# Attention and two MLP layers in one kernel: layer 2 eleven pairs behind layer 1 instead of fifteen, two slot orders, key sums on VectorE alone

## The chip, the core and the metric

The program runs on one core of a Trainium2 chip. The metric is the device time of one execution in microseconds (us). The core has five engines with queues of their own: TensorE (PE, with its weight loads shown apart as PEld), VectorE (DVE), ScalarE (ACT), GpSimd (POOL) and SyncE (SP), which here only issues DMAs. Each engine takes its instructions strictly in the order in which they were written, and an instruction that waits for a semaphore holds up everything behind it on its engine.

## What is computed

```python
kv_pool = kv.reshape(B, H // 4, 4, W // 4, 4, C).mean(axis=(2, 4))   # 12288 rows -> 768 keys
k = v = kv_pool.reshape(B, -1, C) @ w_sr
s = (q @ k.transpose(0, 2, 1)) / np.sqrt(C)
a = np.exp(s - s.max(-1, keepdims=True));  a /= a.sum(-1, keepdims=True) + 1e-09
x = a @ v                                          # 12288 tokens x 128
h = x @ moe_w_in;   x2 = (h * np.clip(h + 3, 0, 6) / 6) @ moe_w_out      # layer 1, d_ff 2048
h = x2 @ moe2_w_in; g = np.where(h >= 1, h, np.where(h <= -1, 0, (h + 1) ** 2 / 4))
out = g @ moe2_w_out                               # layer 2, d_ff 2048
```

The four weight matrices arrive as 64-bit floats, and are turned into 32-bit values on the chip. Every large product is made of three products of a high and a low part (high x high, high x low, low x high), so that each operand is split once into `hi` (a cast on ACT) and `lo` (a subtraction).

## The kernel before

**Units of work.** The 12288 tokens are 24 blocks of 512. In each layer a block has 8 pairs (a pair is 256 columns of d_ff), so that each layer has 192 pairs. A pair of layer 1 is: `m_in(0, s)`, six matmuls on PE into a PSUM tile `h`; `relu1` (ACT); `mul1` (DVE); `hi_lo` (a cast on ACT, a subtraction on POOL); `m_out(0, s)`, six matmuls into the accumulator `acc0`. A pair of layer 2 is: `m_in(1, s)`; `clip2` (DVE, into the buffer `g2`); `sq2` (ACT); `max2` (DVE, the last reader of `h`); `hi_lo` (ACT, POOL); `m_out(1, s)` into `acc1`. There are two `h` tiles and two `g2` buffers. At the end of a block `acc1` is transposed by `o_T` (DVE) and stored; there is one `acc1`, so the next block's first `m_out(1)` waits for `o_T`.

**Attention of a block.** It comes in four parts of 128 queries: `s_mm` (PE), `s_max` (DVE), `s_exp` (ACT), `s_tail_a` (DVE, ACT), `s_tail_b` (DVE and a transposing DMA on SP); `av` (PE) then makes 256 columns of x out of two parts.

**Order.** Nothing is scheduled by a program: the instructions stand as the Python code issues them. First a prologue, a string of steps: `k` sums a tile of 1024 key rows (12 tiles, eight on DVE and four on POOL by `KV_MODE`), `g` finishes the sum on PE, `t p z y` make keys and values, `jN.0` to `jN.3` are the four stages that convert weight piece N (of 16), `s n e a b` are attention of block 0, `x0 x1` its `av`. Then comes one call of `slot(T)` for T = 0, 1, 2, ...: pair T of layer 1, pair T - O2 of layer 2 with O2 = 15, and beside them attention of the next blocks and, at the slots of `CONV_AT`, the conversion of one more weight piece, whose four stages take four slots. `max2` and `hi_lo` of layer 2's pair stand at the start of the next slot. From T = 192 on there is only layer 2. `out2` issues `m_out(1)` two slots behind its `m_in(1)`, and three behind from T = 192 + LAG3_AT on.

**Names and lines** (of the profile): `kv_pool` L235 to L239, `q_T` L325 to L330, `m_in` L416, `m_out` L431, `x2h` and `x2l` L438 and L439, `o_T` L447, `relu1` L460, `mul1` L467, `clip2` L474, `sq2` L481, `max2` L486, `hi_lo` L496 (cast) and L500 (subtraction), `s_tail_b` L379, weight stages L164 to L195.

Of the kernel before, what the change touches and what calls it, by code (L numbers as in the profile page):

```python
# [46 lines left out]
def tile_attn_moe_moe2(  # L47
# [267 lines left out]
    def q_load(b):  # L315
        if b >= NB:
            return
        q_t[b] = q_p.tile([128, BLK], FP32, tag="q", name="q")
# [238 lines left out]
    def slot(T):  # L557
        s1, s2 = T, T - O2
        if ok(s1):
            m_in(0, s1)  # L560
        if ok(s2 - 1) and T < NS:
            max2(s2 - 1)
        if T in tail_at and T > EXP_T:
            s_exp(*tail_at[T])
        if ok(s1):
# [5 lines left out]
        if T < NS:
            out2(T)
        if ok(s1):
            mul1(s1)
# [111 lines left out]
```

## Time and profile before

| | us |
|---|---|
| three runs | 1460.87, 1462.96, 1463.34 (median 1462.96) |
| the profiled execution | 1460.99 |
| its span, first to last instruction | 1459.2 |
| PE, DVE, ACT, POOL busy | 1340.0, 1117.1, 964.2, 1066.1 |

```profile
PE   4658899999999999999999999999999999999665
DVE  7578887778778878878878778788788888766543
ACT  2557777767667667667677677677677677667432
POOL 5267897777777777778778778778778687778433
PEclk9879999999999999999999999999999999999978
DMA  9352222222122122122122212212212212200000
```

Each digit is the busy share of one fortieth of the span (36.5 us) in tenths, 9 being 90% or more; PEclk is the clock that PE was granted, in tenths of full speed. PE is at 9 from the sixth slice to the thirty-seventh; at both ends it is not, and there the clock digit falls as well.

### The profile page before, as it was taken

What the parts mean: (1) busy time and instruction counts of PE and PEld (TensorE: products, weight loads), DVE (VectorE), ACT (ScalarE), POOL (GpSimd) and SP (SyncE); (2) the same over time, 40 slices, a digit from 0 to 9 for tenths busy, and PEclk for the clock granted to TensorE, in tenths of its full rate; (3) what the DMA queues carried; (4) which work ended last, traced back from release to release, by engine and by line L of the source; (5) the groups of instructions that cost most, each with busy time, mean ns of one, the idle gap of its engine ahead of it and who ended that gap; (6) DMA issues with size and microseconds to landing.
All of it is one profiled execution on the core that took longest, in us unless ns stands there. A gap on an engine that the chain in (4) does not pass through costs nothing.

```text
span 1459.2 us, 16720 instructions
## 1 busy us (share of the span) xinstructions
PE 1340.0 (92%) x6123; PEld 1071.1 (73%) x6123; DVE 1117.1 (77%) x1253; ACT 964.2 (66%) x1141; POOL 1066.1 (73%) x485
## 2 busy tenths in 40 slices
PE   4658899999999999999999999999999999999665
PEld 4546677787787787787787787787787787787443
DVE  7578887778778878878878778788788888766543
ACT  2557777767667667667677677677677677667432
POOL 5267897777777777778778778778778687778433
PEclk9879999999999999999999999999999999999978
DMA  9352222222122122122122212212212212200000
GB/s 311 80 119 40 45 46 37 40 40 42 35 40 47 30 40 48 30 40 47 33 37 47 38 32 47 40 30 47 40 30 47 38 24 40 40 12 8 8 7 8
DMA packets 260770, 66.18 MB, mean 45 GB/s; under 512 B 252368, under 2 KB 256592, under 8 KB 260688
## 3 DMA queue, kind: packets, MB, share of 16 engines
q1 hardware_dynamic: 257344, 62.68, 21.8%
q10 hardware_dynamic: 3344, 2.43, 0.6%
q8 instruction: 49, 0.80, 0.2%
q14 instruction: 33, 0.27, 0.1%
HBM read 21.04 MB, written 6.29 MB: 19 GB/s over the span
## 4 chain that ended last, share of the span: by engine, by line
PE 76%; DVE 7%; POOL 3%; ACT 3%; issue 2%; POOLq 0%; DVEq 0%; ACTq 0%
PE acc L431 33%; PE h L416 32%; PE s L342 6%; PE s L394 6%; POOL l L500 3%; DVE g L474 2%; DVE g L486 2%; ACT h L496 1%; DVE o L447 1%; ACT x2h L438 1%; DVE a L379 1%; DVE wa L175 0%; ACT t L460 0%; DVE nm L348 0%; DVE wa L173 0%
## 5 line engine op out<-in xcount | busy, mean ns | idle before, releaser
L500 POOL TENSOR_TENSOR l<-g,h 128x1024 fp32r<-128x1024 f32 (+1 forms) x200 | 459.3, 2298 | 314.9 <-issue 222.0
L500 POOL TENSOR_TENSOR l<-t,h 128x1024 fp32r<-128x1024 f32 (+1 forms) x215 | 531.0, 2474 | 26.8 <-ACT h L496 26.8
L474 DVE TENSOR_SCALAR g<-h 128x1024 f32<-128x1024 f32 (+1 forms) x193 | 234.9, 1218 | 131.5 <-PE h L416 83.6
L467 DVE SCALAR_TENSOR_TENSOR t<-t,h 128x1024 f32<-128x1024 f32 (+1 forms) x193 | 233.9, 1212 | 100.4 <-ACT t L460 100.4
L460 ACT ACTIVATE t<-h 128x1024 f32<-128x1024 f32 (+1 forms) x193 | 196.7, 1020 | 147.0 <-PE h L416 106.1
L481 ACT ACTIVATE g<-g 128x1024 f32<-128x1024 f32 (+1 forms) x193 | 203.6, 1056 | 115.6 <-DVE g L474 114.0
L496 ACT CAST h<-t 128x1024 fp32r<-128x1024 f32 (+1 forms) x193 | 202.1, 1047 | 87.5 <-DVE t L467 84.6
L496 ACT CAST h<-g 128x1024 fp32r<-128x1024 f32 (+1 forms) x193 | 200.4, 1039 | 77.8 <-DVE g L486 75.2
L486 DVE TENSOR_TENSOR g<-h,g 128x1024 f32<-128x1024 f32 (+1 forms) x193 | 232.4, 1205 | 22.6 <-ACT g L481 22.4
L416 PE MATMUL h<-x2h,wi1h 128*128 128x512 f32 x384 | 157.8, 411 | 28.3 <-DVE g L486 25.3
L431 PE MATMUL acc<-h,wo1h 128*128 128x512 f32 x384 | 156.2, 407 | 19.6 <-DVE o L447 18.2
L431 PE MATMUL acc<-l,wo1h 128*128 128x512 f32 x384 | 154.0, 401 | 12.4 <-POOL l L500 12.4
L416 PE MATMUL h<-xh,wi0h 128*128 128x512 f32 x384 | 153.5, 400 | 9.1 <-ACT wi0h L193 8.5
L416 PE MATMUL h<-xh,wi0l 128*128 128x512 f32 x384 | 154.3, 402 | 4.7 <-POOL wi0l L195 4.7
L431 PE MATMUL acc<-l,wo0h 128*128 128x512 f32 x384 | 154.2, 402 | 4.6 <-POOL l L500 4.3
L431 PE MATMUL acc<-h,wo0h 128*128 128x512 f32 x384 | 156.3, 407 | 0.1
L431 PE MATMUL acc<-h,wo1l 128*128 128x512 f32 x384 | 153.9, 401 | 1.4 <-POOL wo1l L195 1.4
L416 PE MATMUL h<-x2l,wi1h 128*128 128x512 f32 x384 | 154.5, 402 | 0.0
L416 PE MATMUL h<-x2h,wi1l 128*128 128x512 f32 x384 | 154.1, 401 | 0.0
L416 PE MATMUL h<-xl,wi0h 128*128 128x512 f32 x384 | 153.8, 400 | 0.0
L431 PE MATMUL acc<-h,wo0l 128*128 128x512 f32 x384 | 152.5, 397 | 0.5 <-POOL wo0l L195 0.5
L379 DVE SCALAR_TENSOR_TENSOR a<-e,rc,a 128x768 f16<-128x768 f32 x96 | 128.6, 1340 | 2.1 <-ACT a L372 2.1
(146 smaller groups left out, 2121.6 us busy)
## 6 DMA issues: line engine op xcount, KB each, us to landing
out_dram<-o SPq DMA_DIRECT2D x96, 64.0 KB, 2.0
q<-in_q_dram SPq DMA_DIRECT2D x92, 64.0 KB, 2.5
h<-in_moe_w_out_dram SPq DMA_DIRECT2D x4, 512.0 KB, 6.5
l<-in_kv_dram SPq DMA_DIRECT2D x4, 512.0 KB, 8.9
h<-in_kv_dram ACTq DMA_DIRECT2D x3, 512.0 KB, 5.5
at<-a SPq DMA_TRANSPOSE x96, 3.6
g<-in_moe_w_in_dram SPq DMA_DIRECT2D x2, 512.0 KB, 5.6
g<-in_kv_dram SPq DMA_DIRECT2D x2, 512.0 KB, 8.7
```

Source lines behind the costliest of these rows:

```text
L342: nc.tensor.matmul(s[:, h, :384], l[:, js], r[:, ks], start=(n == 0), stop=(n == 2))
L379: nc.vector.scalar_tensor_tensor(out=a[:, 1], in0=e, scalar=rc, in1=a[:, 0], op0=ALU.mult, op1=ALU.subtract)
L394: nc.tensor.matmul(ps, l[:, k, :], r[:, k, :], start=(n == 0), stop=(n == 3 * KC - 1))
L416: nc.tensor.matmul(ps[:, k], l[:, ws], r, start=(n == 0), stop=(n == 2))
L431: nc.tensor.matmul(acc[m], l[:, ws], r[:, k, :], start=(c == 0 and i == 0), stop=(c == NPAIR - 1 and i == 5))
L460: nc.scalar.activation(out=g[:, p], in_=h_t[0, s][:, p], func=ACTF.Relu, scale=1.0 / 6.0, bias=0.5)
L467: nc.vector.scalar_tensor_tensor(out=g[:, p], in0=g[:, p], scalar=1.0, in1=h[:, p], op0=ALU.min, op1=ALU.mult)
L474: nc.vector.tensor_scalar(out=g[:, p], in0=h_t[1, s][:, p], scalar1=1.0, scalar2=-1.0, op0=ALU.min, op1=ALU.max)
L481: nc.scalar.activation(out=g[:, p], in_=g[:, p], func=ACTF.Square, scale=0.5, bias=0.5)
L486: nc.vector.tensor_tensor(out=g[:, p], in0=h[:, p], in1=g[:, p], op=ALU.max)
L496: nc.scalar.copy(out=hi[:, p], in_=g[:, p])
L500: eng.tensor_tensor(out=lo[:, p], in0=g[:, p], in1=f32(hi[:, p]), op=ALU.subtract)
```

## The change

- The four key tiles that POOL summed are summed on DVE; the prologue takes the tiles one by one (`k0 g0`, `k1 g1`, ...).
- The queries of block 0 are loaded as plain rows and transposed by four matmuls against the identity into PSUM, with their low part made on DVE; before, they were loaded in pieces of 32 columns and transposed on DVE. Their load stands behind four key tiles instead of ahead of all.
- Weight pieces 4 and 5 are begun in the prologue, and the other ten in slots 0 to 14 (before: 12 pieces in slots 0 to 19).
- O2 is 11 instead of 15. `LAG3_AT` (O2 - 6) and `o_at` follow it.
- Slots 0 to 19 have an order of their own (`early_slot`), in which `max2` stands in its own slot and `m_out(1)` at the slot's end. `slot` serves from 20 on, with `o_T` behind `mul1` instead of at the slot's end, as long as T < 192.
- In the last eleven pairs of layer 2 every second one uses the `t1` buffers for `clip2` instead of `g2`, and from T = 192 on `sq2` stands ahead of `max2` and `hi_lo` of the pair before.

```diff
-O2, LAG2 = 15, 2
+O2, LAG2 = 11, 2
-LOADS = "q0 k0 w k1 k2 k3 w k4 k5 k6 k7 w k8 k9 k10 k11 w q1 w q2 w w w w w w w w w w w"
-KV_MODE = "VVGVVGVVGVGV"
+LOADS = "k0 w k1 k2 k3 q0 w k4 k5 k6 k7 w k8 k9 k10 k11 w w w q1 w w w q2 w w w w w w w"
 PROLOGUE = """
-j0.0 k0 j0.1 k1 k2 g0 g1 t0 p0 j0.2 k3 z0 y0 j1.0 j0.3 k4 k5 g2 g3 t1 p1 j1.1 z1 y1 q0 k6 k7
...
+k0 g0 j0.0 k1 g1 j0.1 t0 p0 k2 z0 y0 g2 j0.2 k3 g3 t1 p1 j1.0 z1 y1 j0.3 k4 g4 q0 k5 g5 t2 p2 j1.1
...
+j2.2 j3.0 j2.3 j3.1 x0 q1 j4.0 x1 j3.2 j4.1 j3.3 j5.0 j4.2
-CONV_AT = (0, 1, 2, 3, 5, 7, 9, 11, 13, 15, 17, 19)
-ACT_T = 24
+CONV_AT = (0, 1, 3, 4, 6, 7, 8, 10, 12, 14)
+EARLY_T = 20
+ACT_T = 20
+ACT_A0 = (0, 1)
...
-        eng = nc.vector if KV_MODE[i] == "V" else nc.gpsimd
-        eng.tensor_tensor(out=t[:, :, 0:2], in0=t[:, :, 0:2], in1=t[:, :, 2:4], op=ALU.add)
+        nc.vector.tensor_tensor(out=t[:, :, 0:2], in0=t[:, :, 0:2], in1=t[:, :, 2:4], op=ALU.add)
...
+        if b == 0:
+            t, tok = new_s()[:, 0], q_t.pop(0)
+            for n in range(4):
+                nc.tensor.transpose(t[:, n * 128:(n + 1) * 128], tok[:, n], ident)
+            nc.scalar.copy(out=hi, in_=t)
+            nc.vector.tensor_tensor(out=lo, in0=t, in1=f32(hi), op=ALU.subtract)
...
     def clip2(s):
-        g = g_t[1, s] = hl_p.tile([128, 2, 512], FP32, tag="g2", name="g2")
+        tag = "t1" if s >= NS - O2 and s % 2 else "g2"
+        g = g_t[1, s] = hl_p.tile([128, 2, 512], FP32, tag=tag, name=tag)
...
+    def early_slot(T):
+        s1, s2 = T, T - O2
+        if ok(s1):
+            m_in(0, s1)
+            relu1(s1)
+        if T in tail_at:
+            s_tail_a(*tail_at[T], on_act=T < ACT_T)
+        mul1(s1)
+        if ok(s2):
+            m_in(1, s2)
+            clip2(s2)
+        if ok(s2 - 1):
+            hi_lo(1, s2 - 1)
+        hi_lo(0, s1)
+        if ok(s2):
+            sq2(s2)
+        if T in s_at:
+            s_mm(*s_at[T])
+            s_max(*s_at[T])
+        if T in tail_at:
+            s_tail_b(*tail_at[T])
+        if ok(s2):
+            max2(s2)
...
+        conv_step(T in CONV_AT)
+        load_next()
+        if ok(s1 - 1):
+            m_out(0, s1 - 1)
+        out2(T)
...
     def slot(T):
...
         if ok(s1):
             mul1(s1)
+        if T in o_at and T < NS:
+            o_T(o_at[T])
         if ok(s2):
             m_in(1, s2)
...
         if ok(s2):
             sq2(s2)
+        if ok(s2 - 1) and T >= NS:
+            max2(s2 - 1)
+            hi_lo(1, s2 - 1)
...
         if T >= NS:
             out2(T)
-        if T in o_at:
-            o_T(o_at[T])
+            if T in o_at:
+                o_T(o_at[T])
```

**Early slots, DVE.** From slot 16 into slot 17 of the kernel before: `t` is `mul1`'s output, `g` that of `clip2` and `max2`, `wa` and `wst` belong to the weight conversion.

```order
L467 SCALAR_TENSOR_TENSOR t_1496<-t_1496,h 128x1024
L474 TENSOR_SCALAR g_1522<-h 128x1024
L348 TENSOR_REDUCE nm<-s 128x1
L173 TENSOR_SCALAR wa<-wa 128x512
L175 TENSOR_SCALAR wa<-wa 128x512
L486 TENSOR_TENSOR g_1522<-h,g_1522 128x1024
L366 TENSOR_SCALAR su<-su 128x1
L369 RECIPROCAL rc<-su 128x1
L467 SCALAR_TENSOR_TENSOR t_1556<-t_1556,h 128x1024
```

The same engine in the changed kernel, from slot 15 into slot 16.

```order
L477 SCALAR_TENSOR_TENSOR t_1284<-t_1284,h 128x1024
L486 TENSOR_SCALAR g_1299<-h 128x1024
L389 SCALAR_TENSOR_TENSOR a<-e,rc,a 128x768
L498 TENSOR_TENSOR g_1299<-h,g_1299 128x1024
L172 TENSOR_SCALAR wa<-wa 128x512
L174 TENSOR_SCALAR wa<-wa 128x512
L477 SCALAR_TENSOR_TENSOR t_1339<-t_1339,h 128x1024
```

`max2` (L486 before, L498 now) stood behind the conversion's DVE instructions and now stands ahead of them.

**Full slots, DVE.** Around an `o_T` (the transpose into `o`) in the middle of the kernel before; `x2l` is the low part of layer 2's input, `nm` is `s_max`.

```order
L467 SCALAR_TENSOR_TENSOR t_5994<-t_5994,h 128x1024
L474 TENSOR_SCALAR g_6018<-h 128x1024
L348 TENSOR_REDUCE nm<-s 128x1
L439 TENSOR_TENSOR x2l<-acc_5643,x2h 128x512
L447 STREAM_TRANSPOSE o<-acc_5595 128x512
L486 TENSOR_TENSOR g_6018<-h,g_6018 128x1024
```

The same in the changed kernel.

```order
L477 SCALAR_TENSOR_TENSOR t_5850<-t_5850,h 128x1024
L457 STREAM_TRANSPOSE o<-acc_5447 128x512
L486 TENSOR_SCALAR g_5880<-h 128x1024
L358 TENSOR_REDUCE nm<-s 128x1
L498 TENSOR_TENSOR g_5880<-h,g_5880 128x1024
```

The transpose has moved ahead of `clip2` and `s_max`, and, as layer 2's block now ends four slots apart from layer 1's, it no longer stands behind `x2l`.

**Last slots, DVE.** `clip2` and `max2` in turn in the kernel before, with the buffers' numbers.

```order
L474 TENSOR_SCALAR g2_11707<-h_11700 128x1024
L486 TENSOR_TENSOR g2_11692<-h_11685,g2_11692 128x1024
L474 TENSOR_SCALAR g2_11729<-h_11722 128x1024
L486 TENSOR_TENSOR g2_11707<-h_11700,g2_11707 128x1024
L474 TENSOR_SCALAR g2_11750<-h_11743 128x1024
```

The same in the changed kernel.

```order
L486 TENSOR_SCALAR g2_11688<-h_11681 128x1024
L498 TENSOR_TENSOR t1_11661<-h_11654,t1_11661 128x1024
L486 TENSOR_SCALAR t1_11703<-h_11696 128x1024
L498 TENSOR_TENSOR g2_11688<-h_11681,g2_11688 128x1024
L486 TENSOR_SCALAR g2_11725<-h_11718 128x1024
```

The order is the same; the outputs take turns between two `g2` and two `t1` buffers.

## Rows read from the trace of the kernel before

**Rows 1.** Windows: us, busy by engine (instructions), PEclk, DMA share, GB/s.

```profile
0.00:60.80 60.80, 32.11 (x135) 27.30 (x135) 40.92 (x71) 21.81 (x43) 23.19 (x24) 0.92 0.83 234
60.80:133.20 72.40, 52.41 (x228) 39.05 (x229) 55.01 (x65) 47.63 (x68) 47.32 (x32) 0.88 0.32 71
133.20:193.60 60.40, 51.35 (x218) 39.03 (x217) 50.71 (x57) 45.06 (x60) 51.05 (x37) 0.92 0.23 44
193.60:279.10 85.50, 81.15 (x380) 64.93 (x379) 68.96 (x76) 60.50 (x71) 70.53 (x40) 1.00 0.21 40
279.10:1350.00 1070.90, 1055.55 (x4945) 854.68 (x4944) 853.68 (x945) 752.16 (x860) 833.17 (x337) 1.00 0.21 37
1350.00:1361.00 11.00, 10.03 (x43) 7.72 (x41) 9.25 (x9) 5.26 (x8) 5.35 (x3) 1.00 0.00 1
1361.00:1439.40 78.40, 46.77 (x150) 30.76 (x150) 32.45 (x29) 26.55 (x28) 30.78 (x13) 0.87 0.04 7
1439.40:1459.20 19.80, 10.63 (x30) 7.66 (x30) 6.08 (x8) 5.25 (x7) 4.75 (x2) 0.76 0.09 14
```

**Rows 2.** Waits of PE, 60 to 224 us: us in total, times, longest.

```profile
PE h L416 <- ACT wi0h L193: 8.5, 2, 4.8
PE h L416 <- DVE g L486: 4.8, 2, 3.8
PE h L416 <- POOL wi0l L195: 4.7, 2, 2.4
```

**Rows 3.** Key sums on DVE by line: ns min/median/max, first and last start.

```profile
L238 DVE TENSOR_TENSOR l<-l x3: 681/1415/1765, 15.6 to 23.3; 128x512 f32<-128x512 f32 x3
...
L239 DVE TENSOR_TENSOR g<-g x3: 424/1371/1400, 8.8 to 31.7; 128x256 f32<-128x256 f32 x3
L239 DVE TENSOR_TENSOR l<-l x3: 424/828/1372, 16.3 to 25.1; 128x256 f32<-128x256 f32 x3
```

**Rows 4.** Timeline of the prologue: start us, us, engine, line, what [idle before <-releaser].

```profile
0.73 2.05 ACTq L320 DMA_DIRECT2D q<-in_q_dram  x4
...
8.07 0.69 DVE L238 TENSOR_TENSOR g<-g 128x512 f32<-128x512 f32 x1 [6.01 <-DMA g<-in_kv_dram]
...
31.66 1.37 DVE L239 TENSOR_TENSOR g<-g 128x256 f32<-128x256 f32 x1
...
60.81 0.50 PE L416 MATMUL h<-xh,wi0h 128*128 128x512 f32 x1 [0.56 <-ACT xh L399]
```

**Rows 5.** Waits of PE, 224 to 1356 us.

```profile
PE acc L431 <- DVE o L447: 15.9, 21, 1.6
```

**Rows 6.** Timeline around one `o_T`, DVE and then PE.

```profile
766.53 1.23 DVE L474 TENSOR_SCALAR g<-h 128x1024 f32<-128x1024 f32 x1 [0.54 <-PE h L416]
...
775.76 0.70 DVE L447 STREAM_TRANSPOSE o<-acc 128x512 f32<-128x512 f32 x1
...
776.61 0.47 PE L431 MATMUL acc<-h,wo1h 128*128 128x512 f32 x1 [0.71 <-DVE o L447]
```

**Rows 7.** Timeline of one pair of layer 2 ahead of T = 192.

```profile
1341.60 0.39 PE L416 MATMUL h<-x2h,wi1h 128*128 128x512 f32 x1
1341.83 0.39 PE L416 MATMUL h<-x2l,wi1h 128*128 128x512 f32 x1
...
1343.28 1.23 DVE L474 TENSOR_SCALAR g<-h 128x1024 f32<-128x1024 f32 x1 [0.55 <-PE h L416]
```

**Rows 8.** Timeline of a slot behind T = 192, all engines.

```profile
1388.65 1.22 DVE L474 TENSOR_SCALAR g<-h 128x1024 f32<-128x1024 f32 x1 [3.69 <-POOL l L500]
...
1389.79 1.21 DVE L486 TENSOR_TENSOR g<-h,g 128x1024 f32<-128x1024 f32 x1
...
1391.09 1.05 ACT L496 CAST h<-g 128x1024 fp32r<-128x1024 f32 x1 [4.04 <-DVE g L486]
...
1391.15 0.47 PE L416 MATMUL h<-x2h,wi1h 128*128 128x512 f32 x1
...
1392.28 2.36 POOL L500 TENSOR_TENSOR l<-g,h 128x1024 fp32r<-128x1024 f32 x1 [3.67 <-ACT h L496]
...
1394.67 1.22 DVE L474 TENSOR_SCALAR g<-h 128x1024 f32<-128x1024 f32 x1 [3.67 <-POOL l L500]
```

**Rows 9.** Timeline of PE at the last pair's `m_in(1)`.

```profile
1440.01 0.63 PE L416 MATMUL h<-x2l,wi1h 128*128 128x512 f32 x1
1440.43 0.63 PE L416 MATMUL h<-x2h,wi1l 128*128 128x512 f32 x1
```

More of the change, by code (lines that the diff above doesn't have):

```diff
@@ L39 @@
 AB = 3
-EXP_T = 11
-HALF_T = 24
 LO_DVE = ((0, 'out', 2),)
@@ L236, in kv_pool @@
         t = kv_t[i][0]
-        eng = nc.vector if KV_MODE[i] == "V" else nc.gpsimd
-        eng.tensor_tensor(out=t[:, :, 0:2], in0=t[:, :, 0:2], in1=t[:, :, 2:4], op=ALU.add)
-        eng.tensor_tensor(out=t[:, :, 0], in0=t[:, :, 0], in1=t[:, :, 1], op=ALU.add)
+        nc.vector.tensor_tensor(out=t[:, :, 0:2], in0=t[:, :, 0:2], in1=t[:, :, 2:4], op=ALU.add)
+        nc.vector.tensor_tensor(out=t[:, :, 0], in0=t[:, :, 0], in1=t[:, :, 1], op=ALU.add)
     def kv_sum_mm(i):
@@ L317, in q_load @@
             return
+        if b == 0:
+            q_t[b] = q_p.tile([128, 4, C], FP32, tag="q", name="q")
+            nc.scalar.dma_start(out=q_t[b], in_=q[0, :BLK].rearrange("(n p) c -> p n c", p=128))
+            return
         q_t[b] = q_p.tile([128, BLK], FP32, tag="q", name="q")
         for a in range(4):
-            (nc.sync if b else nc.scalar).dma_start(
+            nc.sync.dma_start(
                 out=q_t[b][32 * a:32 * a + 32].rearrange("i (b j) -> i b j", j=32), in_=q_v[b, a]
@@ L324, in q_T @@
     def q_T(b):
-        t = q_p.tile([128, BLK], FP32, tag="qT", name="qT")
+        t = q_p.tile([128, BLK], FP32, tag="qT", name="qT") if b else None
         hi = q_p.tile([128, BLK], F32R, tag="qh", name="qh")
         lo = q_p.tile([128, BLK], F32R, tag="ql", name="ql")
+        if b == 0:
+            t, tok = new_s()[:, 0], q_t.pop(0)
[3 more added lines that the diff above has]
+            nc.vector.tensor_tensor(out=lo, in0=t, in1=f32(hi), op=ALU.subtract)
+            qT_t[b] = (hi, lo)
+            return
         nc.vector.transpose(out=t, in_=q_t.pop(b))
@@ L496, in hi_lo @@
             nc.scalar.copy(out=hi[:, p], in_=g[:, p])
-        early = s + (O2 if m else 0) < HALF_T
+        early = s + (O2 if m else 0) < EARLY_T
         for p in (slice(0, 1), slice(1, 2)) if early else parts(m, s):
@@ L553, in out2 @@
             out2_at[0] += 1
-    def slot(T):
+    def early_slot(T):
         s1, s2 = T, T - O2
@@ L560, in slot @@
             m_in(0, s1)
[L561 to L565, printed above, removed]
             relu1(s1)
-        if ok(s2 - 1) and T < NS:
-            hi_lo(1, s2 - 1)
         if T in tail_at:
             s_tail_a(*tail_at[T], on_act=T < ACT_T)
[L571 to L574, printed above, removed]
+        mul1(s1)
         if ok(s2):
             m_in(1, s2)
-        if ok(s1):
-            hi_lo(0, s1)
-        if ok(s2):
             clip2(s2)
-        if ok(s2 - 1) and T >= NS:
-            max2(s2 - 1)
+        if ok(s2 - 1):
             hi_lo(1, s2 - 1)
+        hi_lo(0, s1)
         if ok(s2):
             sq2(s2)
-        if T in tail_at and T >= EXP_T:
-            s_tail_b(*tail_at[T])
         if T in s_at:
@@ L590, in slot @@
             s_max(*s_at[T])
-        if T in tail_at and T < EXP_T:
+        if T in tail_at:
             s_tail_b(*tail_at[T])
-        if T in s_at and T < EXP_T:
+        if ok(s2):
+            max2(s2)
+        if T in s_at:
             s_exp(*s_at[T])
@@ L602, in slot @@
             m_out(0, s1 - 1)
+        out2(T)
+    def slot(T):
+        s1, s2 = T, T - O2
+        if ok(s1):
+            m_in(0, s1)
+        if ok(s2 - 1) and EARLY_T < T < NS:
+            max2(s2 - 1)
+        if T in tail_at and T > EARLY_T:
+            s_exp(*tail_at[T])
+        if ok(s1):
+            relu1(s1)
+        if ok(s2 - 1) and T < NS:
+            hi_lo(1, s2 - 1)
+        if T in tail_at:
+            s_tail_a(*tail_at[T])
+        if T < NS:
+            out2(T)
+        if ok(s1):
+            mul1(s1)
+        if T in o_at and T < NS:
+            o_T(o_at[T])
+        if ok(s2):
+            m_in(1, s2)
+        if ok(s1):
+            hi_lo(0, s1)
+        if ok(s2):
+            clip2(s2)
+        if ok(s2):
+            sq2(s2)
+        if ok(s2 - 1) and T >= NS:
+            max2(s2 - 1)
+            hi_lo(1, s2 - 1)
+        if T in tail_at:
+            s_tail_b(*tail_at[T])
+        if T in s_at:
+            s_mm(*s_at[T])
+            s_max(*s_at[T])
+        if T in av_at:
+            av(*av_at[T])
+        if T in q_at:
+            q_T(q_at[T])
+        if ok(s1 - 1):
+            m_out(0, s1 - 1)
         if T >= NS:
             out2(T)
-        if T in o_at:
-            o_T(o_at[T])
+            if T in o_at:
+                o_T(o_at[T])
     with tc.manual_schedule():
@@ L643, in tile_attn_moe_moe2 @@
             steps[f"e{j}"] = lambda j=j: s_exp(0, j)
-            steps[f"a{j}"] = lambda j=j: s_tail_a(0, j, True)
+            steps[f"a{j}"] = lambda j=j: s_tail_a(0, j, j in ACT_A0)
             steps[f"b{j}"] = lambda j=j: s_tail_b(0, j)
@@ L654, in tile_attn_moe_moe2 @@
         for T in range(NS + O2 + 16):
-            slot(T)
+            (early_slot if T < EARLY_T else slot)(T)
 _INS = ["q", "kv", "w_sr", "moe_w_in", "moe_w_out", "moe2_w_in", "moe2_w_out"]
```

5 lines of the change are left out of this document (2 added, 3 removed).

## The prediction

> **What bounds the kernel now.** I read the windows by stage first [rows 1], cut at the first matmul of slot 0 (60.8 us), slots 11 and 20 (133.2, 193.6), slot 32 (279.1), slot 191 (1350.0), and of layer 2's pairs 182 (1361.0) and 191 (1439.4). Four stages with four different limits are to be seen.
>
> The full slots, 32 to 190, take 1070.9 us for 159 slots. PE is busy for 1055.55 of them at a clock of 1.00; DVE has 80%, ACT 70%, POOL 78%. This is PE's stage. What PE idles there is one wait: the first `m_out(1)` of a block waits for `o_T`, 15.9 us in 21 waits from 224 us on [rows 5]. One of these, 0.7 us like the one in [rows 6], lies ahead of slot 32, so that 15.2 us belong to this stage, all but 0.2 of its idle time.
>
> Slots 0 to 19 take 132.8 us (72.4 + 60.4), 6.64 a slot, though up to slot 15 PE has only one layer. DVE is busy for 55.01 + 50.71 = 105.7 us of it (80%), POOL for 98.4. PE waits in this stretch for weight pieces that are not converted yet, 8.5 + 4.7 = 13.2 us, and 4.8 for `max2` [rows 2]. Slots 20 to 31 take 85.5, 7.1 a slot.
>
> From 1361.0 on only layer 2 is left: 13 pairs in 78.4 us, 6.03 each, with PE at 60%, DVE at 41% and POOL at 39%. Where no engine is full, a ring of waits sets the pace, and one slot shows it [rows 8]: `clip2` starts at 1388.65, `max2` 1.14 later, the cast 1.30 after that, POOL's subtraction 1.19 after the cast, and the next `clip2` 2.39 later, released by that subtraction. Together 6.02. What `clip2` waits for is its buffer: there are two `g2`, and POOL is the last reader.
>
> **The change, part by part.** All terms are against the profiled execution, 1460.99 us (span 1459.2).
>
> *Prologue.* The load of block 0's queries held the ACT queue for 2.05 us ahead of the first key tile, and the first sum started at 8.07 [rows 4]. With the tile in front it can start about 2 us earlier. From there the chain is key sums on DVE to 33.0 (31.66 + 1.37), then 27.8 us of attention of block 0 to slot 0 at 60.8, which keeps its steps. Four tiles move from POOL to DVE, at 0.68 + 0.42 = 1.1 us each at the least [rows 3]: +4.4. The same rows show DVE's eight tiles slowed, with medians of 1.42 and of 0.83 to 1.37 against minima of 0.68 and 0.42. With POOL's four tiles gone fewer of them should be. I take back half of the largest excess, (1.42 - 0.68 + 1.37 - 0.42) / 2 = 0.85 for each of eight: -6.8. Sum -2 + 4.4 - 6.8 = -4.4; I take -4. Ends: +2.4 if the slowing stays, -11 if all of it goes (-2 + 4.4 - 13.5). The four PE transposes and one low part on DVE replace a DVE transpose and a POOL subtraction, beside DMA waits: nothing. The conversion of pieces 4 and 5 goes into the 27.8 us of attention, in the whole prologue DVE is busy only 40.92 of 60.8; if that cover fails, it delays slot 0 by the stages that stand ahead of it, which the end of +2.4 is to hold.
>
> The Trainium skill (SBUF — State Buffer, section SBUF: two separate sides) calls the ports that VectorE and GpSimd share an exclusive lock: a VectorE instruction with two SBUF inputs and a GpSimd instruction that reads SBUF shut each other out for a whole instruction. The durations in [rows 3] fall into two groups as that would have it. By it nearly all of the slowing would go with POOL's tiles, and this term would be near -11; but POOL keeps the conversions, and the sum goes by -4.
>
> *Slots 0 to 19.* Pieces 4 and 5 are done before slot 2, and pieces 6 and 7 by slots 3 and 4, while slots 4 and 6 need them: the 13.2 us should go. Without them DVE's share of the stage was 105.7 / 119.6 = 88%. New is that 9 pairs of layer 2 fall into these slots instead of 5, each 1.22 + 1.21 on DVE [rows 8]: 105.7 + 9.7 = 115.4. `max2` now stands ahead of the conversion, so that `m_in(1)` of the next slot, which needs its `h` tile, is not held by it (the 4.8 us). The new wait is DVE's for the square within the slot: behind it stand the conversion's steps and the next `mul1`, for which ACT and POOL wait; cover is `s_max` or `s_tail_b`. I take a share of 90%: 115.4 / 0.9 = 128.2, with a little for the two pieces still in work at slot 0, 129: -3.8. Ends: 95%, 121.5 (-11), and the 80% of before, 144.3 (+12).
>
> *Slots 20 to 31.* Conversion is over, both layers run; 12 slots at PE's pace, (1070.9 - 15.2) / 159 = 6.64, are 79.7; I take 80: -5.5. Ends: -5.8 and 0.
>
> *Full slots.* `o_T` moves from behind `x2l` to behind `mul1`. In the slots shown `clip2` waited 0.54 us for `m_in(1)`, which PE runs behind the block's last `m_out(1)` [rows 6]: when DVE gets to the new place, `acc1` has been complete for most of the 1.4 us of an `m_in` (6 x 0.23, [rows 7]). So the transpose, 0.70 us, starts at once, and PE needs `acc1` only in the next slot, behind another `m_in(0)`. `clip2` comes 0.70 - 0.54 = 0.16 late, in a slot that has six matmuls of `s_mm` more on PE. The stall of 15.2 goes whole: -15.2. What is late next is PE itself. Ends: -15.2, and +3 (0 gained, 20 times 0.16 lost). The output's four DMAs now stand on SP ahead of the next slot's transposing DMA instead of behind one; only the next block's `o_T` waits for that store.
>
> *The tail.* From T = 192 there are four slots fewer: 4 x 6.03 = -24.1. With four buffers `clip2` no longer waits for POOL. The ring that is left is `h`: `m_in(1)` to `clip2` 1.68 [rows 7], `clip2` to `max2` 1.14, `max2` to the next `m_in(1)` 1391.15 - 1389.79 = 1.36 [rows 8]: 4.18 at full clock. POOL (2.36) and ACT (two passes of 1.05) fit. With PE at 1.2 GHz a matmul comes every 0.42 instead of 0.23 [rows 9, 7]: 5.32. The clock was 0.87 in this stage, a quarter of the time at half; with the same share 4.18 + 0.26 x 1.14 = 4.5. Nine steps (pairs 182 to 191) gain 9 x (6.03 - 4.5) = 13.8. The 11.0 us from slot 191 to pair 182 and the last 19.8 I leave. Term -37.9; ends -24.1 (nothing from the buffers) and -40.8 (4.18).
>
> The Trainium skill (TensorE: Matmul & The Clock Gate, Part 1) has PE's full clock released by recent activity and taken back when it idles. By it the denser tail would run at 2.4 GHz throughout and the term would be -40.8. The trace agrees so far as the clock is 1.00 in the full slots and 0.87 and 0.76 behind them.
>
> *Sum:* -4 - 3.8 - 5.5 - 15.2 - 37.9 = -66.4, so 1394.6 for the profiled execution. The median of the three runs, 1462.96, lies 2.0 higher: 1396.6, rounded 1397.
>
> **Rivals.**
>
> (a) *The tail keeps its 6.03.* For it: DVE's order there is unchanged, two `h` tiles are still all there is. Against: the row's releaser is POOL. 1397 + 13.8 = 1411.
>
> (b) *The early stage gives nothing.* DVE is its fullest engine and gets more work, key sums and four pairs of layer 2. Against: 13.2 us of plain waiting for weights go. Prologue, slots 0 to 19 and 20 to 31 at no gain: 1397 + 13.3 = 1410; at the 80% end 1422.
>
> (c) *The `o_T` stall stays, or turns up at `m_in(1)`.* For it: `m_in(1)` waits for `max2`, and that for a `clip2` that is later. Against: the 0.16. 1397 + 15.2 = 1412.
>
> (d) *Slower: DVE and ACT run in turn in slots 0 to 19.* In the new order a slot's passes follow from one another: `relu1`, `mul1`, `clip2`, `sq2`, `max2`, some 1.05 each on ACT and 1.22 on DVE [rows 8], 5.8; with `s_tail_b` and two instructions of conversion at the held 1.4 of [rows 3], all on DVE in the same line, 10. The other terms gain 62.6; it decides from (132.8 + 62.6) / 20 = 9.8 us a slot on, and at 10 the time is about 1467. Against: `relu1` of the next slot does not wait for `max2`, so half of the line overlaps.
>
> (e) *More than forecast:* every term at its near end, 1460.99 - 83.8 + 2.0 = 1379.
>
> **How the numbers follow.** Chances: forecast (1382 to 1408) 0.61, (a) 0.10, (b) 0.13, (c) 0.08, (d) 0.04, (e) 0.04. About 0.2% (2.9 us) is what a measurement of this kernel can tell from no change. Faster by more: all but (d) and a pile of (a), (b) and (c) at their far ends (1460.99 - 6.7 + 2.0 = 1456 at the worst): 0.95; within 0.2%: 0.01; slower: 0.04. The range of 8 in 10 is 1380 to 1424: it takes in (a), (b) with its far end and (c).
>
> **What would show it.** Right: slot 0 near 57 us, slot 20 near 186, slot 32 near 266; no PE wait for `wi0h` or `wi0l`; no "PE acc <- DVE o" in the full slots; 4.2 to 5.3 us between the `m_in(1)` of the last pairs, with `clip2` released by PE. Wrong: DVE idle in slots 11 to 19 for the square, more than 9 us a slot; `clip2` still released by POOL in the tail; PE waiting for `max2` every eighth slot; PE's clock at half for most of the tail.

## The result, and the profile after

The changed kernel takes 1414.08 us (median of four runs, 1412.91 to 1414.52) against 1461.91 for the kernel before on the same chip: a ratio of 0.967, 95% interval 0.965 to 0.969. It is 47.8 us faster, where 66 were forecast: the sign and the range (1380 to 1424) hold, but the time is 17 us above the forecast of 1397 and outside the 1382 to 1408 that were given 0.61. The profiled execution took 1414.49 us, its span 1412.5.

These are the windows of the kernel after, cut at slots 0, 11, 20, 32 and 191 as in [rows 1], and at layer 2's pairs 182 and 191. In [rows 1] the cut at 1361.0 is pair 178 and not pair 182, as the prediction calls it: with a lag of 15, slot 191 has pair 176. So its window of 78.4 us holds 13 steps, and the one below 9; the columns are us, busy time by engine (instructions), PEclk, DMA share, GB/s.

```profile
0.00:74.10 74.10, 35.13 (x140) 28.82 (x140) 37.25 (x80) 20.49 (x42) 11.73 (x15) 0.93 0.63 184
74.10:143.90 69.80, 55.98 (x228) 43.21 (x229) 58.53 (x72) 49.16 (x71) 51.11 (x36) 0.85 0.36 83
143.90:210.70 66.80, 60.03 (x266) 46.45 (x265) 57.58 (x63) 51.63 (x67) 61.42 (x45) 0.97 0.23 48
210.70:291.00 80.30, 80.20 (x380) 65.14 (x379) 66.31 (x74) 56.54 (x66) 64.31 (x29) 1.00 0.22 40
291.00:1343.00 1052.00, 1051.31 (x4945) 854.72 (x4944) 854.33 (x945) 752.03 (x860) 834.48 (x337) 1.00 0.21 38
1343.00:1354.00 11.00, 10.01 (x43) 7.72 (x41) 9.24 (x9) 6.32 (x9) 5.35 (x3) 1.00 0.01 2
1354.00:1395.10 41.10, 27.46 (x102) 19.55 (x103) 22.52 (x20) 19.46 (x20) 21.37 (x9) 0.96 0.04 7
1395.10:1412.50 17.40, 9.58 (x30) 6.52 (x30) 7.42 (x8) 4.32 (x6) 4.73 (x2) 0.84 0.10 16
```

Against [rows 1], stage by stage:

| stage | us after | change forecast | change measured |
|---|---|---|---|
| prologue, to slot 0 | 74.1 | -4.0 | +13.3 |
| slots 0 to 19 | 136.6 | -3.8 | +3.8 |
| slots 20 to 31 | 80.3 | -5.5 | -5.2 |
| full slots | 1052.0 | -15.2 | -18.9 |
| slot 191 to the end | 69.5 | -37.9 | -39.7 |
| span | 1412.5 | -66.4 | -46.7 |

Two stages of five went the other way than forecast. The prologue lost 13.3 us where 4 were to be gained, 17.3 us off, and slots 0 to 19 lost 3.8 where 3.8 were to be gained, 7.6 off. The full slots and the end gained 5.5 more than forecast, so that 19.7 us are missing in the sum.

**The prologue after.** DVE is busy for 37.25 of 74.1 us, less than the 40.92 of [rows 1], in a longer time. What it waits for until the first score matmul (50.18 us; 36.8 before) is mostly one line: DVE's waits in the kernel after, 0 to 50.2 us (total, times, longest).

```profile
DVE kTl L261 <- ACT kTh L260: 15.6, 5, 6.4
DVE g L236 <- DMA g<-in_kv_dram: 4.0, 1, 4.0
DVE ql L335 <- ACT qh L334: 2.7, 1, 2.7
```

kTh is the high part of the keys, a cast on ACT, and kTl the low part, a subtraction on DVE. A sixth such wait (2.6 us) ends just behind the window: 18.2 in all. In the kernel before there are three, 3.4 us in all (0.44, 0.27 and 2.70), the longest of them in the timeline of its DVE:

```profile
37.08 0.29 DVE L263 SCALAR_TENSOR_TENSOR kTl<-h,kTh 128x128 fp32r<-128x128 f32 x1 [2.70 <-ACT kTh L262]
```

The first wait of the kernel after is followed back in its timeline (start us, us, engine, what, [idle before <-releaser]).

```profile
6.02 0.35 ACTq L652 DMA_DIRECT2D wsr<-in_w_sr_dram  x1
...
18.26 0.77 PE L254 MATMUL h<-e,wsr 128*128 128x128 f32 x2 [7.41 <-DMA wsr<-in_w_sr_dram]
...
19.07 0.28 ACT L260 ACTIVATE kTh<-h 128x128 fp32r<-128x128 f32 x1 [7.91 <-PE h L254]
...
19.38 0.29 DVE L261 SCALAR_TENSOR_TENSOR kTl<-h,kTh 128x128 fp32r<-128x128 f32 x1 [6.42 <-ACT kTh L260]
21.10 0.42 DVE L237 TENSOR_TENSOR h<-h 128x256 f32<-128x256 f32 x1
...
24.25 0.29 DVE L261 SCALAR_TENSOR_TENSOR kTl<-h,kTh 128x128 fp32r<-128x128 f32 x1 [2.73 <-ACT kTh L260]
```

And this is that load in the list of DMA issues (KB, us from issue to landing).

```profile
wsr<-in_w_sr_dram ACTq DMA_DIRECT2D x1, 64.0 KB, 12.1
```

In the kernel before the same load took 7.0 us, and there, too, it was issued behind the query block and four key tiles:

```profile
6.37 0.45 ACTq L610 DMA_DIRECT2D wsr<-in_w_sr_dram  x1
```

So its place on the queue is old; new is that it lands at 18.1 us and not at 13.4. What makes it later was not isolated. The trace shows two differences: the query block, now one load of 256 KB, stands directly ahead of it, and SP's queue issues its second weight piece and its first key tile at 1.21 and 1.68 us, where before it was 5.87 and 6.67.

Read from below: DVE waits for ACT's cast, ACT for the key product on PE, PE for the matrix `w_sr`, which ACT's queue issues at 6.02 us, behind four key tiles and the query block, and which lands 12.1 us later. Meanwhile tiles that have arrived lie there unsummed, since their sums stand on DVE behind the waiting kTl. Later keys have `w_sr`, but the pattern stays: each kTl follows its own tile's sums directly, and DVE waits 1.8 to 2.7 us for the trip over PE and ACT.

**The slots.** Waits of PE in slots 0 to 19 of the kernel after, 74 to 211 us.

```profile
PE s L352 <- ACT e L367: 9.1, 4, 3.9
PE h L426 <- ACT xh L409: 3.5, 2, 2.7
PE acc L441 <- POOL l L511: 3.4, 7, 0.7
PE h L426 <- DVE g L498: 3.1, 3, 1.9
```

The 13.2 us for unconverted weights of [rows 2] are gone, as forecast. At their head stands now a wait that the prediction did not have, score matmuls of the next block's attention behind an exp (4.7 us in three waits in the kernel before, up to slot 20). In the full slots, 291 to 1343 us, all that is left of PE's waits is this line.

```profile
PE h L426 <- DVE g L498: 0.7, 1, 0.7
```

The transpose in its new place, timeline of DVE, answers to [rows 6]: it starts 1.14 us behind `mul1` without a wait.

```profile
747.28 1.22 DVE L477 SCALAR_TENSOR_TENSOR t<-t,h 128x1024 f32<-128x1024 f32 x1
748.42 0.71 DVE L457 STREAM_TRANSPOSE o<-acc 128x512 f32<-128x512 f32 x1
```

**The tail**, timeline of the kernel after, two stretches, answering to [rows 8].

```profile
1363.40 0.39 PE L426 MATMUL h<-x2h,wi1h 128*128 128x512 f32 x1
...
1365.08 1.22 DVE L486 TENSOR_SCALAR g<-h 128x1024 f32<-128x1024 f32 x1 [2.30 <-PE h L426]
1366.22 1.21 DVE L498 TENSOR_TENSOR t<-h,t 128x1024 f32<-128x1024 f32 x1
...
1367.47 1.05 ACT L507 CAST h<-t 128x1024 fp32r<-128x1024 f32 x1
1368.60 2.36 POOL L511 TENSOR_TENSOR l<-t,h 128x1024 fp32r<-128x1024 f32 x1 [2.17 <-ACT h L507]
1371.01 0.50 PE L441 MATMUL acc<-l,wo1h 128*128 128x512 f32 x1 [1.47 <-POOL l L511]
1372.29 0.40 PE L426 MATMUL h<-x2h,wi1h 128*128 128x512 f32 x1
...
1377.46 0.63 PE L426 MATMUL h<-x2h,wi1l 128*128 128x512 f32 x1
...
1381.98 0.47 PE L426 MATMUL h<-x2h,wi1h 128*128 128x512 f32 x1 [1.11 <-DVE g L498]
...
1390.86 0.47 PE L426 MATMUL h<-x2h,wi1h 128*128 128x512 f32 x1 [1.58 <-DVE g L498]
1395.11 0.47 PE L426 MATMUL h<-x2h,wi1h 128*128 128x512 f32 x1 [1.21 <-DVE t L498]
```

`clip2` is now released by PE, no longer by POOL. Nine steps take 41.1 us, 4.57 each, where 4.5 was forecast. They have two limits. Up to 1376 us the ring still goes over POOL, by way of PE's order: `m_in(1)` at 1363.40, `clip2`, `max2` of the pair before, its cast, its subtraction, the `m_out(1)` that waits for it at 1371.01, and behind that on PE an `m_in(1)` at 1372.29: 8.89 for two steps. From T = 197 on `m_out(1)` comes one slot later, and the ring through `h` that the prediction worked out is left: 8.88 for two steps (4.25 and 4.63) and then 4.25 us, PE released by `max2`, against its 4.18. One pair ran at half clock (1377.46, 0.63 each, the granted clock 0.93 from 1376.8 on), and its step is 5.51.

### The profile page after: what moved, and what is told of

It reads as the page before. It is cut to its first block, busy times and chain, and to the rows that moved or that the text cites. A ratio compares the mean times of both kernels' runs of the same rounds, so it can differ in the third digit from the quotient of the medians.

```text
span 1412.5 us, 16726 instructions
## 1 busy us (share of the span) xinstructions
PE 1329.7 (94%) x6127; PEld 1072.1 (76%) x6127; DVE 1113.2 (79%) x1265; ACT 960.0 (68%) x1137; POOL 1054.5 (75%) x472
## 4 chain that ended last, share of the span: by engine, by line
PE 83%; DVE 4%; ACT 2%; issue 1%; POOL 1%; DMA 0%; POOLq 0%; DVEq 0%; ACTq 0%
PE h L426 36%; PE acc L441 35%; PE s L352 6%; PE s L404 6%; DVE g L486 1%; POOL l L511 1%; DVE g L498 1%; ACT t L470 0%; ACT h L507 0%; DVE t L477 0%; DVE t L486 0%; DVE t L498 0%; DVE wa L172 0%; DMA wst<-in_moe_w_out_dram 0%; ACT g L493 0%
## 5 line engine op out<-in xcount | busy, mean ns | idle before, releaser
L511 POOL TENSOR_TENSOR l<-g,h 128x1024 fp32r<-128x1024 f32 (+1 forms) x195 | 450.7, 2313 | 254.6 <-issue 204.4
L511 POOL TENSOR_TENSOR l<-t,h 128x1024 fp32r<-128x1024 f32 (+1 forms) x216 | 540.7, 2507 | 25.1 <-ACT h L507 22.8
L486 DVE TENSOR_SCALAR g<-h 128x1024 f32<-128x1024 f32 x186 | 227.3, 1222 | 68.6 <-PE h L426 66.7
L493 ACT ACTIVATE g<-g 128x1024 f32<-128x1024 f32 x186 | 197.4, 1061 | 116.6 <-DVE g L486 112.7
L507 ACT CAST h<-t 128x1024 fp32r<-128x1024 f32 (+1 forms) x200 | 208.5, 1043 | 96.8 <-DVE t L477 93.7
L498 DVE TENSOR_TENSOR g<-h,g 128x1024 f32<-128x1024 f32 x186 | 225.7, 1213 | 22.7 <-ACT g L493 22.7
L507 ACT CAST h<-g 128x1024 fp32r<-128x1024 f32 x186 | 194.0, 1043 | 4.4 <-DVE g L498 1.6
L426 PE MATMUL h<-x2h,wi1h 128*128 128x512 f32 x384 | 155.9, 406 | 13.2 <-DVE g L498 7.4
```

The source lines that it names most:

```text
L426: nc.tensor.matmul(ps[:, k], l[:, ws], r, start=(n == 0), stop=(n == 2))
L486: nc.vector.tensor_scalar(out=g[:, p], in0=h_t[1, s][:, p], scalar1=1.0, scalar2=-1.0, op0=ALU.min, op1=ALU.max)
L493: nc.scalar.activation(out=g[:, p], in_=g[:, p], func=ACTF.Square, scale=0.5, bias=0.5)
```

## The experiments

Edits are against the changed kernel unless said otherwise. Where there is one execution, kernels are compared by the stages of their traces; where there are four, the ratio to the kernel before is given. Beside the three groups of runs the kernel before took 1460.7 (e1 to e4), 1458.7 (e5 to e8) and 1462.5 us (e9 to e12), so a total of one group is not to be set against one of another to the last microsecond. Six kernels with the same prologue (the changed kernel, e5 to e8, e10) start slot 0 between 73.1 and 74.2 us, and those that keep the lag and order of slots 0 to 19 take 135.9 to 136.6 us for them (e12: 134.4), so that smaller differences say nothing.

### The prologue: the load of w_sr, and the order of sums and keys

**e1**: `w_sr` ahead of the key tiles on ACT's queue.

```diff
-        load_next()
-        nc.scalar.dma_start(out=wsr, in_=w_sr)
+        nc.scalar.dma_start(out=wsr, in_=w_sr)
+        load_next()
```

> The changed kernel with one edit: the load of w_sr is issued ahead of the first key tile instead of behind four of them. Theory W (the first key step waits for w_sr, whose load is issued at 6.02 us and lands at 18.1): the first product with w_sr starts near 11.5 instead of 18.1, everything behind it comes about 6 us earlier, slot 0 near 68 instead of 74.1, time near 1408. Rival V (VectorE, which now makes all key sums, sets the pace of the prologue): its work is the same, slot 0 stays at 74, time 1414. Rival D (the landing of the key tiles sets it): the tiles land 0.2 us later, slot 0 at 74, time 1414.

1406.1 us. The load lands 3.5 us behind its issue, the first product with `w_sr` starts at 11.3 instead of 18.3, the first kTl waits for nothing, the other five as long as ever (2.7, 1.8, 2.0, 2.6, 2.6). Slot 0 starts at 67.2 instead of 74.1: the load's place is 6.9 us of the 13.3.

**e2**: in the prologue's string each tile's sums, on DVE (`k`) and PE (`g`), stand ahead of the keys of the pair before.

```diff
-k0 g0 j0.0 k1 g1 j0.1 t0 p0 k2 z0 y0 g2 j0.2 k3 g3 t1 p1 j1.0 z1 y1
+k0 g0 j0.0 k1 g1 k2 g2 t0 p0 j0.1 k3 g3 z0 y0 t1 p1 k4 g4 j0.2 k5 g5 z1 y1
...
```

> The changed kernel with the same prologue steps in another order: the sums of the next key tiles stand ahead of the step that turns the last two into keys, so that VectorE does not wait out that step. Theory S (VectorE waits 11.8 us in the last five key steps for ScalarE's keys, since nothing stands between the sum and them): most of this goes, and the 6.4 us of the first are partly filled; slot 0 near 64 to 66, time near 1405. Rival V: the same work on VectorE, slot 0 at 74, time 1414. Rival D: slot 0 at 74.

1405.33 us, slot 0 at 67.6. The kTl waits fall to 5.1, 1.5, 1.5, 0, 1.5 and 1.3. The order matters by itself, without any change of DVE's work.

**e3**: both edits.

> Both edits of the two runs before. W and S together: slot 0 at 57 to 61, where the prediction had it (56.8), and the rest of the trace as in the changed kernel, time 1397 to 1402. If only one of them holds: slot 0 at 64 to 68, time 1404 to 1408. Rivals V and D: 74 and 1414.

1403.33 us (1402.68 to 1405.23), ratio 0.961 [0.960, 0.963]; slot 0 at 63.8, 2.8 above what was expected. The shortfall has a row, the timeline of ACT in this kernel:

```profile
16.80 0.28 ACT L260 ACTIVATE kTh<-h 128x128 fp32r<-128x128 f32 x1 [2.95 <-PE h L244]
```

The cast waits for L244, the `g` matmuls of a later tile; four of the six casts do so here. Sums and key products of four key steps lie in one PSUM tile (`h`), in columns of their own, so a `g` pulled forward becomes something the cast has to wait for. That sharing the tile is the reason is read from the code and was not isolated. The next edit lets only the DVE sums go ahead.

**e9**: `w_sr` first, and only `k` ahead, `g` behind the keys of the pair before; some conversion steps and the queries' step (`q0`) move along.

```diff
-k0 g0 j0.0 k1 g1 j0.1 t0 p0 k2 z0 y0 g2 j0.2 k3 g3 t1 p1 j1.0 z1 y1
+k0 g0 j0.0 k1 g1 t0 p0 k2 j0.1 k3 z0 y0 g2 g3 t1 p1 k4 k5 z1 y1 j0.2 j1.0 g4 g5 t2 p2
...
```

> The kernel of e3_both with the prologue steps in a third order: only VectorE's sums stand ahead of the key step before, PE's sum matmuls and the queries' low part no longer. Theory G (in e3_both ScalarE's keys wait for the sum matmuls that were written ahead of them, as they share the PSUM tile, 1.5 us in four steps, and VectorE 2.7 us for the queries' high part): these 8 us go mostly, slot 0 at 57 to 60 instead of 63.8, time 1396 to 1400. Rival D (the key tiles' landing sets it now): slot 0 stays at 63 to 64, time 1403.

1399.3 us (1399.17 to 1399.68), ratio 0.957 [0.956, 0.959], the best version, some 14 us below the changed kernel by the two ratios. Slot 0 starts at 61.2, 1.2 later than expected. DVE's waits up to this kernel's first score matmul (0 to 37.3 us), and its first window:

```profile
DVE g L236 <- DMA g<-in_kv_dram: 4.7, 1, 4.7
DVE h L236 <- DMA h<-in_kv_dram: 3.2, 3, 1.4
DVE ql L335 <- ACT qh L334: 2.1, 1, 2.1
...
DVE kTl L261 <- ACT kTh L260: 1.2, 1, 1.2
```

```profile
0.00:61.20 61.20, 33.85 (x140) 28.27 (x140) 36.60 (x80) 20.40 (x42) 11.37 (x15) 0.92 0.76 222
```

The same 80 instructions on DVE, 36.60 us busy against 37.25, and 12.9 us less time. Of 18.2 us of waits for kTh 4.4 are left (1.2 here, and 3.27 that end at 37.58, just behind the window), none of the casts waits for L244, and up to the score matmul DVE waits most for the key tiles themselves. From the first score matmul to slot 0 it takes 23.9 us here as in the changed kernel (24.0 before); all of the loss lay ahead of it. Slot 0 is back where it was (60.8 before), not 4 us earlier.

### The prologue: is it who sums the tiles?

**e4**: four tiles on POOL again, as before.

```diff
+KV_MODE = "VVGVVGVVGVGV"
...
-        nc.vector.tensor_tensor(out=t[:, :, 0:2], in0=t[:, :, 0:2], in1=t[:, :, 2:4], op=ALU.add)
+        eng = nc.vector if KV_MODE[i] == "V" else nc.gpsimd
+        eng.tensor_tensor(out=t[:, :, 0:2], in0=t[:, :, 0:2], in1=t[:, :, 2:4], op=ALU.add)
...
```

> The changed kernel with four key tiles summed on GpSimd again (as before the change), order and all else as changed. Theory S (a chain, not VectorE's work): a GpSimd sum takes 2.2 to 2.7 us against 1.1, and it lies in the chain, so slot 0 comes 2 to 5 us later, 76 to 79, time 1416 to 1419. Rival V: 4.4 us of work leave VectorE, slot 0 near 70, time near 1410.

1413.4 us, slot 0 at 74.0, s0 at 50.2 as in the changed kernel. Neither theory's time came: where the sums run changes nothing that can be told from noise while DVE waits for kTh (16.5 us in five waits here).

**e11**: the same in e9, where most of those waits are gone.

> The kernel of e9_keys_ahead2 with four key tiles summed on GpSimd. With the waits gone from VectorE's queue its own work may count. Theory S (the chain through the sums counts): GpSimd's sums take 2.2 to 2.7 us against 1.1 and hold VectorE's additions, slot 0 1 to 4 us later than in e9_keys_ahead2. Rival V (VectorE's work counts): 2 to 4 us earlier.

1401.98 us, slot 0 at 63.1 against 61.2 in e9: here the place of the sums counts for 1.9 us, in one trace of each, where equal prologues differ by up to 1.1; the whole execution is 2.7 us longer than e9's median. Sums on VectorE alone are worth a little, once the order lets them.

### Slots 0 to 19

**e8**: one slot order throughout, `slot` from T = 0 on with the conversion step added.

```diff
-            (early_slot if T < EARLY_T else slot)(T)
+            slot(T)
```

> The changed kernel with the order of the full slots in slots 0 to 19 too (max2 and the cast of layer 2 in the next slot, behind the conversion; the exponential in the next slot; m_out(1) behind m_in(0)). Theory E (max2 ahead of the conversion is worth something): PE waits for max2 again, slots 0 to 19 take 140 to 148 us instead of 136.6, time 1418 to 1426. Rival I (VectorE is full at either order): 135 to 138, time 1413 to 1416. Rival R (waiting for the square within the slot costs more than it saves): under 134, time under 1412.

1419.88 us. Slots 0 to 19 take 143.7 instead of 136.6. Waits of PE in this kernel, 73 to 218 us:

```profile
PE s L352 <- ACT e L367: 11.4, 4, 5.6
PE h L426 <- DVE g L498: 7.3, 3, 3.4
```

`max2` is back as what PE waits for (3.1 us in the changed kernel). The new order is worth 7.1 us here, `max2`'s place 4.2 of it by this line; the other moves were not taken apart.

**e12**: e9 with more of the conversion of pieces 3 to 5 ahead of the last `av` of block 0.

```diff
-j2.2 j3.0 j2.3 j3.1 x0 q1 j4.0 x1 j3.2 j4.1 j3.3 j5.0 j4.2
+j2.2 j3.0 j2.3 j3.1 j4.0 j3.2 j4.1 x0 q1 j3.3 j4.2 j5.0 x1
```

> The kernel of e9_keys_ahead2 with the conversion of weight pieces 3 and 4 ahead of the first av instead of behind it, where VectorE waits for the transposing DMAs. Theory C (behind the second av these instructions stand ahead of slot 0's mul1, so that slots 0 and 1 take 13 us instead of the 9 of the kernel before): slot 2 comes 9 to 10 us behind slot 0 instead of 13, time 3 us less than e9_keys_ahead2, 1393 to 1397. Rival M (the work is only moved): slot 0 later by what slots 0 and 1 gain, same time.

1401.59 us (1400.2 to 1401.84), ratio 0.959 [0.957, 0.960]: no gain. Slot 0 starts at 63.3 us, 2.1 later than in e9, slot 2 1.0 us earlier (72.4 against 73.4), and by slot 8 both stand level again (114.9 and 114.5). What levels them was not isolated.

### The lag, and the place of o_T

**e7**: lag 15 again, everything else as in the changed kernel.

```diff
-O2, LAG2 = 11, 2
+O2, LAG2 = 15, 2
```

> The changed kernel with layer 2 fifteen pairs behind again. Theory T (a pair of layer 2 moved out of the tail is paid for in the early slots): the tail has four steps of 4.57 us more, +18.3; slots 0 to 31 have four pairs of layer 2 less, 9.8 us of VectorE's work at a share of 85%, -11; time 1419 to 1424. Rival K (the early slots have room, the lag is worth its whole tail): slots 0 to 31 as in the changed kernel, time 1432. Rival N (the lag is worth nothing): 1414.

1422.77 us. This kernel's windows, from slots 0, 32 and 191 on:

```profile
74.20:202.30 128.10, 104.89 (x445) 79.85 (x446) 107.64 (x126) 93.01 (x130) 100.84 (x72) 0.91 0.32 70
...
282.60:1334.70 1052.10, 1051.41 (x4945) 855.68 (x4944) 852.82 (x945) 751.41 (x860) 834.42 (x337) 1.00 0.21 38
1334.70:1421.00 86.30, 58.25 (x223) 41.14 (x221) 49.21 (x46) 38.43 (x41) 40.92 (x18) 0.97 0.06 10
```

The lag of 11 saves 16.8 us at the end (86.3 to 69.5) and costs 8.5 at the start (128.1 to 136.6): the four pairs of layer 2 that leave the tail come in again in slots 0 to 19, with 8.5 us more of DVE work (107.64 to 116.11). At the old lag these slots take 128.1 us against the 132.8 of the kernel before: all other edits together gain 4.7 there, and the lag takes more than that back.

**e6**: `o_T` at the slot's end again.

```diff
-        if T in o_at and T < NS:
-            o_T(o_at[T])
...
-            if T in o_at:
-                o_T(o_at[T])
+        if T in o_at:
+            o_T(o_at[T])
```

> The changed kernel with o_T at the end of its slot again. Theory P (its place in the slot is what counts): the stall of PE comes back once a block, 0.7 us idle and about 0.95 us in all, 20 times in slots 32 to 190, which go from 1052.0 to about 1071; time 1433. Rival L (the lag of 11 is what counts, since o_T no longer falls into the slot with layer 2's input): no stall or a smaller one, slots 32 to 190 at 1052 to 1058, time 1414 to 1420.

1412.44 us, full slots 1052.1 (289.9 to 1342.0). No stall returned: the prediction's reason, the new place, is not needed.

**e10**: both undone, lag 15 and `o_T` at the slot's end.

> The changed kernel with layer 2 fifteen pairs behind and o_T at the end of its slot. Theory X (either of the two edits alone removes PE's stall, since it needs both: o_T late in the slot, and the slot also carrying layer 2's input): the stall is back, 0.7 us idle once a block in slots 32 to 190, which take 1068 to 1072 us instead of 1052.1; time 1440 to 1443. Rival Y (something else in the changed kernel removed it): 1052, time 1423.

1440.31 us. Full slots 1070.5 (282.3 to 1352.8); waits of PE in this kernel, 290 to 1345 us:

```profile
PE acc L441 <- DVE o L457: 15.4, 20, 1.6
```

Four kernels make a square. With lag 11 the full slots take 1052.0 and 1052.1 (place new, place old), with lag 15 1052.1 and 1070.5. Either edit alone removes the stall; the second adds nothing.

### The buffers of the tail

**e5**: two `g2` buffers throughout.

```diff
-        tag = "t1" if s >= NS - O2 and s % 2 else "g2"
+        tag = "g2"
```

> The changed kernel with clip2 on the two g2 buffers throughout, as before the change. Theory B (the four buffers broke the ring through GpSimd): the nine steps from layer 2's pair 182 to pair 191 go back from 4.57 to about 6.03 us, 54 instead of 41.1 us, and the end behind them from 17.4 to 19.8; time 1427 to 1430. Rival O (the square ahead of max2, or the clock, is what made the last slots fast): steps near 4.6, time 1414.

1428.6 us. Pairs 182 to 191 take 54.1 us (1352.9 to 1407.0), 6.01 each, as in [rows 8]. Timeline of DVE in this kernel's tail:

```profile
1374.26 1.23 DVE L486 TENSOR_SCALAR g<-h 128x1024 f32<-128x1024 f32 x1 [3.56 <-POOL l L511]
```

`clip2` is again released by POOL's subtraction, as in the next step. The buffers are worth 13.0 us (54.1 less 41.1), where the prediction had 13.8, and the end behind takes 19.6 instead of 17.4. The granted clock of the nine steps is 0.87 here and 0.96 with the buffers. `sq2` keeps its new place in this kernel, so that alone gains nothing; what it adds beside the buffers was not run.

## Why the prediction was right or wrong, point by point

- **Prologue: wrong, and the step that failed.** The prediction said "From there the chain is key sums on DVE to 33.0" and priced it by DVE's work: tiles added, slowed instructions taken back. The end of the sums was a fact of the order before, where the next tiles' sums stood ahead of each key step. The change took the tiles one by one (`k0 g0 ... k1 g1 ... t0 p0 ... z0`), and each low part of the keys then had to be waited out with the next sums behind it; and the load of `w_sr`, last of the loads ahead of ACT's work as before, landed 4.7 us later. The working asked nothing of either, though the order was in the diff. One part of the term came: the first sum begins at 6.02 instead of 8.07. But up to the first score matmul DVE is busy 21.7 us instead of 25.8 and waits 25.7 us instead of 8.2, 14.9 of the difference for kTh. Measured +13.3 in place of -4: 6.9 by the load (e1), 6.5 by the order (e2), 10.3 by these two edits together (e3), 12.9 with the load and an order that moves only DVE's sums (e9), without a change in DVE's work. The 4 us of gain came in no run. The upper end of that term, +2.4, held the slowing of DVE's instructions and a conversion in the way, so it was no bound on the order of waits.
- **Slowed key sums: the mechanism is there, its worth was not.** With POOL's tiles gone, ten of DVE's twelve second sums run in 0.42 us, as at 21.10 above; before it was three of eight. The three slow sums that are left, of 24, each overlap a conversion on POOL (at 11.00, 25.37 and 45.38 us, with POOL busy from 10.69, 24.83 and 44.84). The size was misread: the durations of DVE's eight tiles before add up to 15.8 us, 7.0 over their minima, and not the 13.5 that two medians of three gave for the end of -11. Twelve tiles take 16.0 us, +0.3 where 4.4 - 6.8 = -2.4 was priced. Summing on DVE then gained nothing in the changed kernel's order (e4) and 1.9 us in e9's (e11). The rule of the Trainium skill on the ports that VectorE and GpSimd share (SBUF — State Buffer, section SBUF: two separate sides) agrees with these overlaps; two groups of durations, as the prediction read [rows 3], are not there, since a second sum also took 0.83 us. By it alone the term near -11 was wrong, since DVE's busy time was not what the prologue waited for.
- **Slots 0 to 19: work right, share wrong, and with it the sign.** DVE's work came to 58.53 + 57.58 = 116.1 us (forecast 115.4), the weight waits went, and the order is worth 7.1 (e8). But DVE's share was 85%, not 90%: at the old lag the stage gained 4.7, and the four pairs of layer 2 cost 8.5 (e7). 3.5 of the 7.6 us above the forecast lie in slots 0 and 1 alone, which take 12.4 us (74.1 to 86.5; 8.9 before), with conversion steps ahead of the first `mul1` and a wait of PE of 3.9 us for an exp. Moving those steps forward (e12) gained nothing by slot 8.
- **Slots 20 to 31: right**, 80.3 for 80: PE's pace.
- **`o_T`: the stall went, the reason was half of it.** The stall went whole, and the stage gained 18.9, more than the near end of 15.2; but the lag alone would have done it (e6), and the place alone as well (e7). That layer 2's block now ends four slots apart from layer 1's is said ahead of the prediction, but was not counted as a cause. A stall also costs more than its idle time: e10 against e6 has 18.4 us for 20 stalls, 0.92 each, of which 15.4 / 20 = 0.77 is PE's wait; another 3.7 us lies in PE's busy time (1055.13 in e10 against 1051.41 in e6). The stall of [rows 6] shows where, in PE's timeline: three matmuls around it start at 775.51, 776.61 and 776.92, 1.41 us where two steps of 0.23 would do. The trace calls 0.71 of that idle; the rest is the first one's whole 0.39, which otherwise lies under its successor, and a slower start behind the stall.
- **Tail: right, its step in part by luck.** Buffers 13.0 for 13.8, a step of 4.57 for 4.5, releaser PE as forecast; the last 19.8 us, left alone in the prediction, became 17.4. The ring of 4.18 is there in the last steps (4.25 in the last); in the first half PE's order ties `m_in(1)` to POOL's subtraction, at 4.5, which the prediction did not see. The clock it assumed to get 4.5 was too low: the granted clock was 0.96 over the nine steps, and with that its own working gives 4.18 + 0.08 x 1.14 = 4.27. The rule of the Trainium skill (TensorE: Matmul & The Clock Gate, Part 1), that recent activity releases the full clock, is borne out in direction: 0.87 in [rows 1] and in e5's nine steps, 0.96 in the denser tail. Full clock throughout, which the prediction read from it, did not come: one pair ran at half.
- **The lag** was priced at 24.1, four steps of 6.03 gone from the tail. With the shorter step they are worth 16.8, and 8.5 come back in the early slots (in the prediction, 9.7 of DVE work): 8.3 net (e7).
- **The rivals.** The time lies beside (a), (b) and (c), at 1411, 1410 and 1412, and only (b), the early stage gives nothing, has the place right: prologue and slots 0 to 19 lost 17.1 us. Its reason, DVE's load, holds for slots 0 to 19 (e7); the prologue's 13.3 us are waits. That the time still fell into the range is luck in part: no rival had the prologue longer, and 5.5 us more than forecast came back in the full slots and the end. (a) and (c) fell by the step of 4.57 and the missing stall; for (d) a slot took 6.8 us, not 9.8.

## What to carry to other kernels

When a change reorders a prologue or a pipeline, go through the new order on each in-order engine and ask of every instruction how far back on that engine its producer's input was made; a step that needs a trip over two other engines belongs behind work that is already at hand. Do the same for each DMA queue: a small tensor that the first product needs goes ahead of the large tiles. And when a stall can go for two reasons, price neither edit by it before both single edits have been run.

## What the runs showed that was not expected

- One 64 KB load took 12.1 us from issue to landing behind four 512 KB tiles and a query block, 7.0 in the kernel before at the same place, 3.5 us as the first of the same queue (e1).
- Where matmuls were pulled forward into a PSUM tile that another engine still had to read, that reader waited for them (e3: 2.95 us at 16.80), though they write other columns.
- A PE stall of 0.77 us on the mean cost 0.92 us of time; the rest appeared as PE busy time.
